# Layer 1 of the experts in seven block products for eight, in a sliding-window attention and dense expert kernel

## Chip, cores and metric

The kernel runs on 1 core of one Trainium2 chip. The metric is the device time of one execution in microseconds (us). A run is compared with runs of the kernel before on the same chip. All runs named here are of state "fast", or single executions counted as such by the measurement; no slow run is used.

## The reference

```python
def reference(...):
    attn = _attn_ref(q, k, v)        # B 8, H 8, S 576, D 64; window 128, ALiBi bias, softmax
    x = attn.transpose(0, 2, 1, 3).reshape(4608, 512)
    return _moe_ref(x, w_gate, w1, w2)

def _moe_ref(x, w_gate, w1, w2):     # N 4608 tokens, D 512, E 8 experts, F 1024
    P = np.exp(x @ w_gate - ...)     # then 8 rounds of row and column scaling (Sinkhorn)
    out = 0
    for e in range(E):
        h = np.maximum(x @ w1[e], 0.0)      # layer 1: 512 -> 1024
        out += P[:, e:e + 1] * (h @ w2[e])  # layer 2: 1024 -> 512
    return out
```

Every token passes through every expert, so nearly all of the time is matmul.

## The kernel before

Attention and most of expert 0 come first. Then 63 *steps* follow: experts 1 to 7, nine groups of 512 tokens each. A step does layer 2 of its own group and, between those products, layer 1 of the next step's group. P scales x before layer 1 (`make_xs`), which is allowed because P is positive.

Layer 2 already uses the Strassen-Winograd form: a 2x2 block product with seven block products for eight, paid for with additions of blocks. These are the sums `S` of h and `T` of w2, on VectorE. The results are gathered in an odd way: all products that several quadrants share go into quadrant (1,1), the others are kept as differences from it, and in the last expert (1,1) is added back (`settle`).

```python
def make_xs(i):                        # VectorE, two instructions of 128x1024
    ... xss[i] = xT[group] * Pb

def l1s(i, ft):                        # layer 1, direct: one eighth of a group
    psh = mps.tile([P, GT], FP32, tag="psh", bufs=3)
    for dt in range(NDT):              # 4 matmuls of 512 columns
        nc.tensor.matmul(out=psh, lhsT=w1ts[e][:, dt, P*ft : P*ft+P],
                         rhs=xss[i][:, dt, :], start=(dt == 0), stop=(dt == NDT - 1))
    nc.scalar.activation(out=hTs[i][:, ft, :], in_=psh, func=AF.Relu)

def product(i, m): ...                 # one of 7 products of layer 2: 8 matmuls of 256 columns

def gather(i, bank, rh, ch, op):
    t = quad(g, rh, ch)
    if (rh, ch) != (1, 1) and e < E - 1:         # far: ScalarE copies, a DMA adds
        st = msb.tile([P, 2, HF], FP32, tag="st", bufs=5)
        nc.scalar.copy(out=st, in_=banks[bank])
        nc.gpsimd.dma_start(out=t, in_=st, accum_op=ALU.add)
        return
    nc.vector.tensor_tensor(out=t, in0=t, in1=banks[bank], op=op)

for i, (e, g) in enumerate(steps):
    make_s(i, 1); product(i, 1); piece()         # piece(): l1s of step i + 1
    make_s(i, 2); gather(i, 0, 1, 1, ALU.add)
    product(i, 7); piece(); make_s(i, 4); gather(i, 1, 1, 1, ALU.subtract)
    product(i, 5); piece(); gather(i, 2, 1, 1, ALU.subtract)
    product(i, 6); piece(); gather(i, 3, 1, 1, ALU.add)
    make_xs(i + 2)
    # ... products 2, 4, 3 with pieces between them, gathers to the other quadrants ...
    if g == NG - 2: make_t(e + 1)                # four sums of w2, once per expert
```

The softmax here doesn't subtract the row's maximum and nothing guards it: scores larger than these inputs give would overflow.

## Time and profile before

| | before |
|---|---|
| median of 13 executions | 1089.14 us (1087.56 to 1090.73) |
| span of the profiled execution | 1086.9 us |
| before step 0 / steps 0 to 60 / the rest | 261.9 / 795.1 / 29.9 us |
| one step | 13.02 us; 13.14 us in the last seven of these steps |

A step is measured in the timeline from the start of its product 1 to the start of the next step's. The third row splits the span at product 1 of step 0 and of step 61.

The busy times on the profile's page, as time, share of the span and number of instructions:

```profile
PE 1051.8 (97%) x7675; PEld 672.5 (62%) x7675; DVE 694.2 (64%) x1072; ACT 543.2 (50%) x959; POOL 270.6 (25%) x264
```

Some of the page's costliest groups: busy time, mean ns of one, then the idle time of the engine just before them and what ended it. Matmuls are pipelined, so the busy time divided by the count is nearer their cost than the mean.

```profile
L580 ACT ACTIVATE hT<-psh 128x512 f16<-128x512 f32 x504 | 302.3, 600 | 424.3 <-PE psh L573 422.7
L573 PE MATMUL psh<-xs,w1t 128*128 128x512 f16 x2016 | 506.3, 379 | 0.2 <-DVE xs L560 0.2
...
L648 DVE TENSOR_TENSOR acc_lo<-acc_lo,M 128x512 f32<-128x512 f32 x186 | 127.2, 684 | 61.6 <-PE M L631 61.6
L560 DVE TENSOR_TENSOR xs<-xT,Pb 128x1024 f16<-128x1024 f16 x126 | 148.2, 1219 | 0.8 <-DMA Pb<-PTd 0.8
```

ScalarE and VectorE wait for TensorE here; the layer-1 matmuls waited 0.2 us in all. Product 1 of three successive steps in the timeline (start, length, engine, line, operation; every second row with this name is product 2 and is left out):

```profile
600.45 1.04 PE L631 MATMUL M<-w2t,hT 128*128 128x256 f16 x8
...
613.47 1.04 PE L631 MATMUL M<-w2t,hT 128*128 128x256 f16 x8
...
626.49 1.04 PE L631 MATMUL M<-w2t,hT 128*128 128x256 f16 x8
```

They lie 13.02 us apart. The table by windows for one step gives each engine's busy time in it, with its number of instructions, then granted clock, DMA share and GB/s:

```profile
601.39:614.41 13.02, 13.02 (x90) 8.60 (x89) 7.43 (x10) 6.12 (x11) 3.57 (x4) 1.00 0.50 83
```

The columns are PE, PEld, DVE, ACT, POOL. TensorE is busy all the time, VectorE for 7.43 us.

### The profile page before, as it was taken

Reading aid. Unit: us, or ns where it says so; the run is one execution under the profiler, and the core shown is the slowest. Engines: PE = TensorE matmul, PEld = TensorE weight load, DVE = VectorE, ACT = ScalarE, POOL = GpSimd, SP = SyncE. Lnnn points to the kernel's source line nnn. Section 1 sums busy time; section 2 is a strip of 40 time slices with the busy share of each in tenths; the row PEclk is TensorE's granted clock in tenths of the full one; section 3 lists DMA queues with packets and bytes.
Section 4 is the critical chain, followed back from the end, with each engine's and each line's share of the span. In section 5 each row is a group of like instructions: output and inputs, shape, how many; then the busy total and the mean of one; then the engine's idle time right before and its main releaser. Section 6 shows DMA issues by size and latency. Waiting matters only on the chain.

```text
span 1086.9 us, 18767 instructions
## 1 busy us (share of the span) xinstructions
PE 1051.8 (97%) x7675; PEld 672.5 (62%) x7675; DVE 694.2 (64%) x1072; ACT 543.2 (50%) x959; POOL 270.6 (25%) x264
## 2 busy tenths in 40 slices
PE   4999999899999999999999999999999999999996
PEld 2555555445666666666666666666666666666664
DVE  5877676556666755565555655565556555667885
ACT  3566666455666544444444444444444444443331
POOL 6333320010223332223222322332222322220000
PEclk9999999899999999999999999999999999999999
DMA  9977871415444595448544765559444944443323
GB/s 168 153 75 78 76 71 9 71 21 121 83 83 79 91 160 87 81 78 146 88 78 79 123 124 84 85 84 162 78 78 78 154 80 83 83 61 105 104 92 96
DMA packets 123334, 101.36 MB, mean 93 GB/s; under 512 B 46288, under 2 KB 107120, under 8 KB 123248
## 3 DMA queue, kind: packets, MB, share of 16 engines
q0 software_dynamic: 107968, 73.44, 50.5%
q1 hardware_dynamic: 14848, 26.34, 7.9%
q8 instruction: 60, 0.98, 0.4%
q10 hardware_dynamic: 432, 0.39, 0.1%
q14 instruction: 26, 0.21, 0.1%
HBM read 79.02 MB, written 9.58 MB: 82 GB/s over the span
## 4 chain that ended last, share of the span: by engine, by line
PE 93%; DVE 2%; DMA 1%; ACT 1%; issue 1%; DVEq 0%; POOL 0%; ACTq 0%; SPq 0%; POOLq 0%
PE psh L573 40%; PE M L631 35%; PE psh L110 6%; PE psy L124 5%; PE psS L218 3%; PE psN L266 2%; ACT pt L226 1%; PE psT_q L187 1%; PE psT_k L187 1%; DMA qf<-in_q_dram 1%; PE psXT L306 1%; DVE xsb L275 0%; DMA PTd<-PT_sb 0%; DVE acc_hi L648 0%; DVE QZ L206 0%
## 5 line engine op out<-in xcount | busy, mean ns | idle before, releaser
L580 ACT ACTIVATE hT<-psh 128x512 f16<-128x512 f32 x504 | 302.3, 600 | 424.3 <-PE psh L573 422.7
L573 PE MATMUL psh<-xs,w1t 128*128 128x512 f16 x2016 | 506.3, 379 | 0.2 <-DVE xs L560 0.2
L573 PEld LDWEIGHTS <-w1t 128*128 128x128 f16 x2016 | 197.3, 98 | 145.7 <-issue 0.5
L631 PEld LDWEIGHTS <-S 128*128 128x128 f16 x2016 | 197.3, 98 | 75.7
L597 DVE TENSOR_TENSOR S<-hT 128x1024 f16<-128x1024 f16 x126 | 86.8, 689 | 198.8 <-ACT hT L580 198.8
L646 POOL DMA_DIRECT2D acc_lo<-st x108 | 128.8, 1211 | 339.4 <-ACT st L645 338.7
L631 PEld LDWEIGHTS <-hT 128*128 128x128 f16 x1512 | 147.9, 98 | 59.3 <-issue 3.1
L648 DVE TENSOR_TENSOR acc_lo<-acc_lo,M 128x512 f32<-128x512 f32 x186 | 127.2, 684 | 61.6 <-PE M L631 61.6
L560 DVE TENSOR_TENSOR xs<-xT,Pb 128x1024 f16<-128x1024 f16 x126 | 148.2, 1219 | 0.8 <-DMA Pb<-PTd 0.8
L631 PE MATMUL M<-w2t,S 128*128 128x256 f16 x1008 | 130.6, 273 | 0.0
L631 PE MATMUL M<-w2t,hT 128*128 128x256 f16 x1008 | 130.6, 273 | 0.0
L631 PE MATMUL M<-T,S 128*128 128x256 f16 x1008 | 130.5, 273 | 0.0
L646 POOL DMA_DIRECT2D acc_hi<-st x54 | 64.4, 1204 | 170.1 <-ACT st L645 167.7
L645 ACT COPY st<-M 128x512 f32<-128x512 f32 x162 | 93.9, 580 | 0.0
L648 DVE TENSOR_TENSOR acc_hi<-acc_hi,M 128x512 f32<-128x512 f32 x93 | 63.6, 684 | 29.3 <-PE M L631 29.0
L226 ACT ACTIVATE pt<-psS 128x1024 f16<-128x1024 f32 (+2 forms) x80 | 68.2, 852 | 17.9 <-PE psS L218 16.8
L110 PE MATMUL psh<-xT,w1t 128*128 128x512 f16 x288 | 72.2, 393 | 1.6 <-ACT P_sb L298 1.1
L124 PE MATMUL psy<-w2t,hT 128*128 128x512 f16 x288 | 66.6, 379 | 0.8 <-ACT P_sb L298 0.8
L631 PE MATMUL M<-T,hT 128*128 128x256 f16 x504 | 65.3, 273 | 1.2 <-DVE acc_hi L648 1.2
L117 ACT ACTIVATE hT<-psh 128x512 f16<-128x512 f32 x72 | 43.1, 598 | 27.1 <-PE psh L110 26.4
L218 PE MATMUL psS<-QZ,KT 128*128 128x512 f16 (+2 forms) x160 | 46.6, 374 | 8.0 <-ACT pt L226 7.2
L234 DVE TENSOR_TENSOR pt<-pt,maskT 128x1024 f16<-128x1024 f16 (+2 forms) x80 | 46.0, 575 | 5.6 <-ACT pt L226 5.4
(61 smaller groups left out, 639.3 us busy)
## 6 DMA issues: line engine op xcount, KB each, us to landing
acc_lo<-st POOLq DMA_DIRECT2D x108, 256.0 KB, 3.9
Pb<-PTd SPq DMA_DIRECT2D x63, 256.0 KB
acc_hi<-st POOLq DMA_DIRECT2D x54, 256.0 KB, 3.9
w2t<-in_moe_w_dram POOLq DMA_DIRECT2D x8, 1024.0 KB, 15.9
w1t<-in_moe_w_dram POOLq DMA_DIRECT2D x7, 1024.0 KB, 9.8
out_dram<-acc_lo SPq DMA_DIRECT2D x48, 128.0 KB
kf<-in_k_dram POOLq DMA_DIRECT2D x16, 288.0 KB, 6.1
qf<-in_q_dram POOLq DMA_DIRECT2D x16, 288.0 KB, 7.0
```

Source lines behind the costliest of these rows:

```text
L110: nc.tensor.matmul(out=psh, lhsT=w1t[:, dt, P * ft : P * ft + P], rhs=xT[:, dt, GT * g : GT * g + GT], start=(dt == 0), stop=(dt == NDT - 1),)
L124: nc.tensor.matmul(out=psy, lhsT=hT[:, ft, P * ms : P * ms + P], rhs=w2ts[e][:, ft, :], start=(ft == 0), stop=(ft == NFT - 1),)
L218: nc.tensor.matmul(out=ps[0:nk, jj, :, 0:nq], lhsT=KT[:, 2 * half + jj, k0 : k0 + nk], rhs=QZ[:, 2 * half + jj, :, k0 : k0 + nq],)
L226: nc.scalar.activation(out=pt[0:nk, :, 0:nq], in_=ps[0:nk].rearrange("p a b q -> p (a b) q")[:, :, 0:nq], func=AF.Exp, scale=scale,)
L560: nc.vector.tensor_tensor(out=xss[i][:, 2 * d2 : 2 * d2 + 2, :], in0=xT[:, 2 * d2 : 2 * d2 + 2, GT * g : GT * g + GT], in1=Pb.unsqueeze(1) ...
L573: nc.tensor.matmul(out=psh, lhsT=w1ts[e][:, dt, P * ft : P * ft + P], rhs=xss[i][:, dt, :], start=(dt == 0), stop=(dt == NDT - 1),)
L580: nc.scalar.activation(out=hTs[i][:, ft, :], in_=psh, func=AF.Relu)
L597: nc.vector.tensor_tensor(out=t, in0=a, in1=b, op=op)
L631: nc.tensor.matmul(out=ps[:, ms, :], lhsT=a[:, kt, P * ms : P * ms + P], rhs=b[:, kt, :], start=(first and ms == 0 and kt == 0), stop=(kt ...
L645: nc.scalar.copy(out=st, in_=banks[bank])
L646: nc.gpsimd.dma_start(out=t, in_=st, accum_op=ALU.add)
L648: nc.vector.tensor_tensor(out=t, in0=t, in1=banks[bank], op=op)
```

## The change

Layer 1 gets the Strassen-Winograd form too. Its cost per step on TensorE falls from 32 matmuls of 512 columns to 56 of 256, seven eighths. The price: three differences of x and one made in place, per step; three sums of w1 and one in place, per expert; and inside each half of layer 1, two copies by ScalarE (one from PSUM to PSUM) and two additions from PSUM by VectorE. Around it much is rearranged so that VectorE keeps up. The core of the diff, with cuts:

```diff
-        def l1s(i, ft): ...                       # direct layer 1
+        def make_xd(i, n):                        # differences of x, 128x512 fp16
+            out, a, b = {
+                1: (xd[:, 0], x_quad(i, 0, 1), x_quad(i, 0, 0)),
+                2: (xd[:, 1], x_quad(i, 1, 1), xd[:, 0]),
+                3: (x_quad(i, 0, 1), x_quad(i, 1, 1), x_quad(i, 0, 1)),
+                4: (xd[:, 2], x_quad(i, 1, 0), xd[:, 1]),
+            }[n]
+            nc.vector.tensor_tensor(out=out, in0=a, in1=b, op=ALU.subtract)
+        def make_ws(e, n): ...                    # four sums of w1, 128x1024 fp16
+        def l1_product(i, dp, m): ...             # 4 matmuls of 256 columns
+        def l1_chunk(i, n):
+            dp, c = divmod(n, 4)
+            if c == 0:
+                l1_product(i, dp, 1)              # bank la
+                nc.scalar.copy(out=lbanks["lb"], in_=lbanks["la"])
+                l1_product(i, dp, 5)              # bank ld
+                m5 = msb.tile([P, 2, T2], FP32, tag="st", bufs=NST)
+                nc.scalar.copy(out=m5, in_=lbanks["ld"])
+            elif c == 1:
+                l1_product(i, dp, 6)              # adds onto the copy in lb
+                l1_product(i, dp, 2)
+                nc.vector.tensor_tensor(out=lbanks["lc"], in0=lbanks["lb"], in1=m5s[i], op=ALU.add)
+                l1_relu(i, dp, lbanks["la"], 0, 0)
+            elif c == 2:
+                l1_product(i, dp, 7)
+                l1_product(i, dp, 3)
+                nc.vector.tensor_tensor(out=m5s[i], in0=lbanks["lb"], in1=m5s[i], op=ALU.add)
+                l1_relu(i, dp, lbanks["lc"], 0, 1); l1_relu(i, dp, m5s[i], 1, 1)
+            else:
+                l1_product(i, dp, 4)
+                l1_relu(i, dp, lbanks["lb"], 1, 0)
...
-                st = msb.tile([P, 2, HF], FP32, name=f"st{bank}_{e}_{g}", tag="st", bufs=5)
+            st = msb.tile([P, 2, HF], FP32, name=f"st{bank}_{e}_{g}", tag="st", bufs=NST)  # NST = 6
...
+            # the last expert too goes by ScalarE and DMA, except its last two steps;
+            # make_t and make_ws are spread over three steps at each expert change;
+            # rescaling and rebasing of expert 0 are spread over the first steps;
+            # P is transposed and sent earlier, within expert 0's layer 1
```

The copy of product 5 (`m5`) shares the staging buffers `st` with the far adds.

## The prediction

> **What bounds the kernel now.** TensorE. It is busy for 97% of the span (the page's busy times), the chain of waits that ended last is 93% PE, and from 300 to 1000 us PE is busy 100.00 of every 100 us at a granted clock of 1.00 (the table by windows). That stretch holds steps (7 experts x 9 token groups = 63). In the timeline one step takes 13.02 us (S1 of two successive steps: 601.39 and 614.41). Its PE part: 32 matmuls of 512 columns for layer 1, eight in 1.73 us, so 6.93 us; 56 of 256 columns for layer 2, eight in 0.87 us, so 6.08 us. VectorE is 58 to 67% busy there, ScalarE 43 to 58%.
>
> **What the change does.** Layer 2 already uses seven block products for eight; now layer 1 does too. Per step, 32 matmuls of 512 columns become 56 of 256.
> - Removed: 6.93 - 56 x 0.1085 = 0.85 us of PE per step, about 53 us in all, entirely on the critical path. Layer 2's narrower matmuls cost no more per column (0.1085 against 0.2165 us).
> - Added on VectorE, per step: four 128x512 fp16 differences of x (0.41 us each, estimated from the mask multiplies of 1024 elements, 0.683 us, and 768, 0.550 us) and four fp32 128x512 additions from PSUM (like the gather: 0.684 us). Back to back, an instruction starts 0.60 us after one of 0.684 us, so the load becomes about 11.1 us in a step of 12.15 us: 91%.
> - Added on ScalarE: four copies of 0.58 us per step; load about 8.5 of 12.15 us.
> - Added per expert: four 128x1024 sums of w1 on VectorE, 0.69 us each.
> - Moved: P is sent earlier; first-expert rescaling is spread out; last-expert adds mostly go through ScalarE and DMA.
>
> The Trainium skill ("VectorE: DVE Perf Modes", Mode 2x_1P) says tensor_tensor on packed 16-bit data gives two results per cycle; this trace agrees: 1024 fp16 elements take 0.69 us, 512 fp32 elements 0.68 us.
>
> **How much arrives.** I walked one ordinary step through the queues with these durations. Each PSUM addition gates a later TensorE product into the same bank, with 0.3 to 0.4 us to spare; VectorE idles about 1 us per step. So ordinary steps should stay bound by PE at about 12.15 us. Given back: six expert changes (VectorE full for three steps each) 3 to 6 us; the last expert, two settling additions per step, 3 to 4 us; the last-but-one step, seven extra VectorE operations, 3 to 4 us; the first step's layer 1, half of it with nothing to interleave, 2 to 3 us. Together 12 to 15 of 53 us.
>
> **Predicted time: 1050 us, range 1041 to 1067.** Chances: faster by over 2% 0.87, within 2% 0.11, slower 0.02.
>
> **What would show it.** Steps of 12.1 to 12.3 us in the middle; PE still 98 to 100% busy from 300 to 950 us; about 9190 PE matmuls; VectorE busy about 960 us (over 90%), ScalarE about 700 us; PE waits on VectorE under 0.3 us per ordinary step, larger at expert changes and in the last expert.
>
> **What would make it wrong.** PSUM-to-PSUM additions slower than 0.684 us, or dependent VectorE operations that don't overlap: then VectorE becomes the limit, steps take 12.4 to 13 us, and the time 1055 to 1085 us. POOL's descriptor work could hold up the DMA adds and the staging buffers. A lower granted clock would also cost.

## The result

| | before | after |
|---|---|---|
| median | 1089.14 us, 13 executions | 1058.33 us, 8 executions (1053.95 to 1060.54) |
| span of the profiled execution | 1086.9 us | 1053.0 us |
| before step 0 / steps 0 to 60 / the rest | 261.9 / 795.1 / 29.9 us | 261.5 / 758.7 / 32.8 us |
| ordinary step | 13.02 us | 12.22 us |
| TensorE / VectorE / ScalarE busy | 1051.8 / 694.2 / 543.2 us | 1003.3 / 923.3 / 692.1 us |

The ratio is 0.9709, 95% interval 0.9693 to 0.9725. Such a ratio is the mean time of one kernel's fast runs over that of the other's of the same rounds, so it is not quite the ratio of the medians above. The outputs are correct. The profiled execution took 1054.86 us and is one of the quicker ones.

The same lines of the page, after:

```profile
PE 1003.3 (95%) x9187; PEld 815.3 (77%) x9187; DVE 923.3 (88%) x1566; ACT 692.1 (66%) x1249; POOL 322.8 (31%) x310
...
L563 DVE TENSOR_TENSOR xs<-xT,Pb 128x1024 f16<-128x1024 f16 x126 | 153.3, 1217 | 0.0
L620 PE MATMUL la<-xs,w1t 128*128 128x256 f16 x1008 | 151.2, 273 | 0.7 <-DVE xs L563 0.7
...
L656 DVE TENSOR_TENSOR lc<-lb,m 128x512 f32<-128x512 f32 x126 | 87.9, 697 | 33.2 <-PE lb L620 28.7
L735 DVE TENSOR_TENSOR acc_lo<-acc_lo,M 128x512 f32<-128x512 f32 x163 | 110.8, 680 | 0.2
```

VectorE's idle time before the gathers (L735) has shrunk from 61.6 to 0.2 us; what it still waits for is mainly the layer-1 bank `lb` of the first PSUM addition. Product 1 of three ordinary steps:

```profile
623.46 1.04 PE L723 MATMUL M<-w2t,hT 128*128 128x256 f16 x8
...
635.68 1.04 PE L723 MATMUL M<-w2t,hT 128*128 128x256 f16 x8
...
647.91 1.04 PE L723 MATMUL M<-w2t,hT 128*128 128x256 f16 x8
```

Now 12.22 and 12.23 us lie between them, 112 matmuls of 0.109 us. The table by windows for three kinds of step: an ordinary one, the second at an expert change, and one of the last expert.

```profile
635.68:647.91 12.23, 12.23 (x114) 10.96 (x112) 11.26 (x19) 8.22 (x17) 3.60 (x3) 1.00 0.57 93
598.17:611.01 12.84, 12.54 (x114) 10.86 (x112) 12.63 (x22) 8.76 (x18) 6.57 (x6) 1.00 1.10 174
957.69:970.19 12.50, 12.43 (x115) 10.96 (x113) 12.28 (x21) 8.32 (x17) 3.60 (x3) 1.00 0.73 148
```

In the ordinary step TensorE is busy throughout and VectorE is idle for 0.97 us. In the other two VectorE has hardly any idle time left and TensorE waits. At an expert change that wait looks like this in the timeline (square brackets: idle time before, and what ended it):

```profile
606.88 0.42 DVE L584 TENSOR_TENSOR xd<-xs 128x512 f16<-128x512 f16 x1
607.22 0.68 DVE L703 TENSOR_TENSOR T<-w2t,T 128x1024 f16<-128x1024 f16 x1
607.96 1.03 PE L723 MATMUL M<-T,hT 128*128 128x256 f16 x8 [0.30 <-DVE T L703]
```

The third sum of w2 is late because VectorE's queue is full. From the step starts, the time lost against 12.22 us in the profiled execution is: 2.9 us in step 0 (15.11 us); 7.3 us at six expert changes (0.9 us at four of them, 2.2 at the first, 1.5 at the last); 1.35 us in five steps of the last expert (12.50 us each); 0.3 us in the other steps of expert 1; and about 1 us in three steps that follow a step with weight loads. The rest, from the start of step 61 on, is 2.9 us longer than before.

### The profile page after: what moved, and what is told of

Same layout as the page of the kernel before. It is cut to its first block, busy times and chain, and to the rows that moved or that the text cites. A ratio compares the mean times of both kernels' runs of the same rounds, so it can differ in the third digit from the quotient of the medians.

```text
span 1053.0 us, 22956 instructions
## 1 busy us (share of the span) xinstructions
PE 1003.3 (95%) x9187; PEld 815.3 (77%) x9187; DVE 923.3 (88%) x1566; ACT 692.1 (66%) x1249; POOL 322.8 (31%) x310
## 5 line engine op out<-in xcount | busy, mean ns | idle before, releaser
L635 ACT ACTIVATE hT<-lc 128x512 f16<-128x512 f32 x126 | 75.4, 598 | 138.5 <-PE lc L620 131.0
L620 PEld LDWEIGHTS <-ws 128*128 128x128 f16 x1512 | 147.3, 98 | 20.4 <-DVE ws L598 1.7
L620 PE MATMUL la<-xs,w1t 128*128 128x256 f16 x1008 | 151.2, 273 | 0.7 <-DVE xs L563 0.7
L723 PE MATMUL M<-T,hT 128*128 128x256 f16 x1008 | 130.6, 273 | 4.9 <-DVE T L703 2.4
L635 ACT ACTIVATE hT<-la 128x512 f16<-128x512 f32 x126 | 75.6, 600 | 72.7 <-PE la L620 72.7
L656 DVE TENSOR_TENSOR lc<-lb,m 128x512 f32<-128x512 f32 x126 | 87.9, 697 | 33.2 <-PE lb L620 28.7
L735 DVE TENSOR_TENSOR acc_lo<-acc_lo,M 128x512 f32<-128x512 f32 x163 | 110.8, 680 | 0.2
L663 DVE TENSOR_TENSOR m<-lb,m 128x512 f32<-128x512 f32 x126 | 86.2, 684 | 2.8 <-PE lb L620 2.8
L635 ACT ACTIVATE hT<-lb 128x512 f16<-128x512 f32 x126 | 75.8, 602 | 8.3 <-PE lb L620 7.2
L635 ACT ACTIVATE hT<-m 128x512 f16<-128x512 f32 x126 | 78.7, 625 | 1.7
L647 ACT COPY lb<-la 128x512 f32<-128x512 f32 x126 | 71.8, 570 | 9.0 <-PE la L620 1.6
```

Of the source, the lines that this page charges most:

```text
L620: nc.tensor.matmul(out=ps[:, f, :], lhsT=a[:, kt, f0 : f0 + P], rhs=b[:, kt, :], start=(first and f == 0 and kt == 0), stop=(kt == 1), ski ...
L635: nc.scalar.activation(out=hTs[i][:, f0 : f0 + 2, T2 * th : T2 * th + T2], in_=src, func=AF.Relu)
L647: nc.scalar.copy(out=lbanks["lb"], in_=lbanks["la"])
L656: nc.vector.tensor_tensor(out=lbanks["lc"], in0=lbanks["lb"], in1=m5s[i], op=ALU.add)
L663: nc.vector.tensor_tensor(out=m5s[i], in0=lbanks["lb"], in1=m5s[i], op=ALU.add)
L723: nc.tensor.matmul(out=ps[:, ms, :], lhsT=a[:, kt, P * ms : P * ms + P], rhs=b[:, kt, :], start=(first and ms == 0 and kt == 0), stop=(kt ...
```

## Experiments

Twelve runs were made, of eleven new kernels and of the changed one again. Each was timed against the kernel before. My theory: ordinary steps are still bound by TensorE, VectorE has about 1 us to spare in each, and what is missing was lost where VectorE has extra work. The rivals: VectorE, 92% busy in an ordinary step (11.26 of 12.23 us), now sets the pace everywhere; or the gain came from the rearranging and not from the seven products.

### direct_l1: the new schedule with the old layer 1

```diff
         def l1_chunk(i, n):
-            ...                                  # seven products
+            psh = mps.tile([P, GT], FP32, name=f"psh_{e}_{g}_{n}", tag=LB[n % 4])
+            for dt in range(NDT):
+                nc.tensor.matmul(out=psh, lhsT=w1ts[e][:, dt, P * n : P * n + P],
+                                 rhs=xss[i][:, dt, :], start=(dt == 0), stop=(dt == NDT - 1))
+            nc.scalar.activation(out=hTs[i][:, n, :], in_=psh, func=AF.Relu)
         # make_xd and make_ws return at once
```

> The changed schedule with layer 1 as before: 32 direct matmuls of 512 columns per step, no x differences, no w1 sums, no additions from PSUM. If the seven-product form of layer 1 makes the gain, the steps go back to 13.02 us and the time to 1085 to 1092 us, ratio 0.995 to 1.003. Rival: the gain comes from what was moved (P sent earlier, the last expert's adds given to ScalarE and DMA, rescaling spread): then a good part of the 31 us stays and the time is under 1075 us. Here a settle of the tail may even cost 2 to 4 us.

Measured: correct, 1090.04 us, ratio 1.0003 (0.9981 to 1.0024). One step by windows:

```profile
601.07:614.09 13.02, 13.02 (x90) 8.61 (x89) 7.95 (x11) 6.70 (x12) 4.80 (x5) 1.00 0.61 101
```

All 61 steps take 13.02 us, those of the last expert too (13.14 us before). The part after step 61 is 32.0 us, against 29.9 us before; up to TensorE's last matmul it is 21.3 us, against 20.7 us. So the rearranging alone brings nothing in total. The rival that credits the rearranging falls. No run has the new layer 1 in the old order, so whether the rearranging was needed is not shown.

### light_x: VectorE relieved (wrong results on purpose)

```diff
         def make_xd(i, n):
+            if i > 1:
+                xds[i] = xds[i % 2]
+                return
```

> Wrong results on purpose: the differences of x are made for the first two steps only, so 1.3 to 1.6 us of VectorE work leaves every later step, and TensorE does the same products. If ordinary steps are bound by TensorE, they stay at 12.22 us, and only the places where VectorE is full gain: about 0.9 us at each of six expert changes and 0.27 us in each of the last expert's steps, together 6 to 10 us, time 1047 to 1052 us. Rival: VectorE, at 93% busy, sets the pace; then every step shortens by 0.5 us or more and the time falls below 1030 us.

Measured: wrong as intended, 1051.91 us, ratio 0.9654 (0.9634 to 0.9673). One ordinary step:

```profile
623.12:635.34 12.22, 12.22 (x114) 10.96 (x112) 9.91 (x15) 8.31 (x17) 3.59 (x3) 1.00 0.59 95
```

VectorE's load fell from 11.26 to 9.91 us and the step stayed at 12.22 us: VectorE does not set the pace of an ordinary step. The steps at four of the expert changes became 12.22 or 12.23 us, and so did those of groups 2 to 7 of the last expert. That shows where a full VectorE cost time. But five steps, each the one after the step in which the next expert's weights were loaded, took 0.3 to 2.0 us more, 6.1 us in all, which I had not expected. One of them:

```profile
840.27 0.57 ACT L650 COPY lb<-la 128x512 f32<-128x512 f32 x1
...
843.59 0.59 ACT L654 COPY m<-ld 128x512 f32<-128x512 f32 x1 [2.75 <-DMA acc_lo<-st]
844.21 0.70 DVE L659 TENSOR_TENSOR lc<-lb,m 128x512 f32<-128x512 f32 x1 [3.17 <-ACT m L654]
...
844.96 0.60 PE L623 MATMUL lb<-xs,w1t 128*128 128x256 f16 x4 [1.86 <-DVE lc L659]
```

ScalarE cannot copy product 5, because its staging buffer is still held by a DMA add that has not landed. VectorE waits for the copy and TensorE for VectorE. This is the shared buffer pool of the diff. DMA adds took 4.9 us (median) and up to 14.2 us to land in this run.

### heavy1 and heavy2: VectorE loaded

```diff
+            def extra():
+                if 2 <= e <= 6 and 1 <= g <= 6:          # 30 ordinary steps
+                    for _ in range(1):                   # heavy2: 2
+                        nc.vector.tensor_tensor(out=P_sb, in0=P_sb, in1=P_sb, op=ALU.max)
             gather(i, 0, 1, 1, ALU.add)
+            extra()
...
                 gather_far(i, 0, 0, 0)
+            extra()
             chunk(5)
```

> Two idle-filling operations of VectorE (0.46 us each alone, about 0.38 us back to back) added to each of 30 ordinary steps (token groups 1 to 6 of experts 2 to 6), one before each first PSUM addition, where I saw VectorE wait. If VectorE has about 0.9 us to spare per step, these steps stay at 12.22 to 12.30 us and the time moves by 0 to +3 us. Rival (VectorE sets the pace): each step grows by 0.76 us, +23 us.

> Twice as many: four such operations, about 1.5 us, in each of the 30 ordinary steps. More than the spare time of about 0.9 us, so the steps should grow by 0.4 to 0.7 us each, +12 to +21 us. Rival (VectorE sets the pace): +1.5 us per step, +46 us. If VectorE had much more to spare than I read: no change.

Measured: heavy1 1059.50 us, ratio 0.9721 (0.9694 to 0.9749); heavy2 1077.97 us, ratio 0.9891 (0.9864 to 0.9919); both correct. One loaded step of each by windows, heavy1 first:

```profile
636.66:648.88 12.22, 12.22 (x114) 10.96 (x112) 11.98 (x21) 8.21 (x17) 3.60 (x3) 1.00 0.59 93
```

```profile
634.59:647.55 12.96, 12.59 (x114) 10.93 (x112) 12.72 (x23) 8.39 (x16) 3.59 (x3) 1.00 0.60 95
```

In heavy1 the loaded steps stay at 12.22 or 12.23 us, but for two that follow weight loads (12.76 and 12.57 us; the changed kernel has such steps too). Each extra operation moves what follows by 0.48 us, so the two of a step add 0.96 us and just fill VectorE's waits. In heavy2 most loaded steps take 12.97 us, 0.75 us more, where I had expected 0.4 to 0.7 us. There two extra operations push the next addition 0.86 us back:

```profile
637.72 0.94 DVE L800 TENSOR_TENSOR P_sb<-P_sb 128x288 f32<-128x288 f32 x2
638.58 0.69 DVE L656 TENSOR_TENSOR lc<-lb,m 128x512 f32<-128x512 f32 x1
639.33 0.60 PE L620 MATMUL lb<-xs,w1t 128*128 128x256 f16 x4 [0.21 <-DVE lc L656]
```

So 1.72 us were added per step, and 0.75 us came out. The spare time was about 0.97 us, which is VectorE's idle time in the ordinary step of the changed kernel, as the prediction's walk had it ("about 1 us"). Past that, TensorE stands before exactly the product that the PSUM addition gates. Together, light_x, heavy1 and heavy2 rule out that VectorE sets the pace in ordinary steps, and show that it is close to doing so.

### spread and st7: the late DMA adds

```diff
-            if g == 0 and 1 < e < E - 1:          # spread: whole w1 and w2 loads in group 0
-                load_w1(...); load_w2(...)
+            if 0 <= g < 4 and 1 < e < E - 1:      # a quarter of each in groups 0 to 3
+                nc.gpsimd.dma_start(out=w1ts[e + 1][:, g : g + 1], in_=...)
+                nc.gpsimd.dma_start(out=w2ts[e + 1][:, 2 * g : 2 * g + 2], in_=...)
```

```diff
-        NST = 6                                   # st7
+        NST = 7
...
-                t = msb.tile([P, KT2, T2], FP16, name=f"S{n}_{e}_{g}", tag=f"S{n}")
+                t = msb.tile(..., tag="S2" if n == 2 else "S34")   # S3 and S4 share a buffer
```

> The changed kernel, correct, with the loads of an expert's w1 and w2 cut into four parts each, one pair in each of the steps of token groups 0 to 3, in place of two whole loads in group 0. Theory: the changed kernel's runs (1054 to 1060.5 us) differ because a DMA add behind a weight load holds a staging buffer, for which ScalarE's copy of the fifth product, and then TensorE, wait (in the trace 1 us of such waits in the profiled run of the changed kernel, more in the slower ones). Then the waits of ScalarE on DMA go away, the median falls to 1053 to 1056 us and the runs lie within 3 us. Rival: the spread has another cause (clock, chip): median 1057 to 1060 and the spread as before.

> The changed kernel, correct, with seven staging buffers in place of six (room made by letting two of the layer-2 sums share one buffer). If staging buffers held by late DMA adds cost time, one more takes most of the wait: ScalarE's waits on DMA under 2 us, median 1054 to 1057 us. Rival: no effect of the number of buffers, 1057 to 1060 us. If the shared buffer adds a wait in ordinary steps, they would show over 12.23 us.

Measured, both correct: spread 1057.28 us (1056.49 to 1057.78), ratio 0.9708 (0.9695 to 0.9722); st7 1054.91 us (1053.93 to 1055.88), ratio 0.9687 (0.9674 to 0.9700). In the changed kernel ScalarE waited for DMA before the copy of product 5 for 3.3 us in all. In spread no such wait is left and the longest landing is 8.7 us, where the changed kernel has 13.2 us; in st7 none is left before that copy, though 2.9 us remain before the copies of the far adds (I had expected under 2 us). Both shorten steps 0 to 60 by 0.8 us, from 758.7 to 757.9 us. So the mechanism is right, but it is worth about 1 us. The median of spread missed my range and lies in the rival's, though its four runs lie within 1.3 us. In its profiled execution the time before step 0 was 265.0 us, where st7 had 262.0 us and the changed kernel 261.5 us, with the same program up to there. Most of the spread between runs is therefore not the late adds. The traces show where these 3.5 us arise: early in the attention, in spread's stretch from 40 to 47 us, the granted clock is 0.50 and a 128x512 matmul takes 0.62 us, where the changed kernel has 1.00 and 0.38 us; the 201st to the 400th matmul take 22.2 us in spread and 19.7 us there. The matmuls of 0.62 us end at 39 to 40 us in four of the fourteen traces (the changed kernel, st7, best3, settle_pool) and at 47 to 50 us in the other ten. What ends them is not shown.

### settle_pool: the last expert's additions on GpSimd

```diff
-            nc.vector.tensor_tensor(out=t, in0=t, in1=quad(g, 1, 1), op=ALU.add)
+            eng = nc.vector if g == NG - 1 else nc.gpsimd
+            eng.tensor_tensor(out=t, in0=t, in1=quad(g, 1, 1), op=ALU.add)
```

> The changed kernel, correct, with the last expert's settling additions on GpSimd in place of VectorE, but for the last token group. If the last expert's steps take 12.50 us because VectorE is full, they fall to 12.23 to 12.30 us, and the last step starts earlier by up to 2.6 us: 2 to 5 us in all, median 1053 to 1056 us. Rival: GpSimd is too slow at it or hinders VectorE; then the VectorE operations beside it take longer and the steps stay at 12.5 us or grow.

Measured: correct, 1076.92 us, ratio 0.9889 (0.9870 to 0.9909). The rival was right, and by more than I had thought. The steps of the last expert take 13.65 to 17.14 us once these additions begin. From the timelines of VectorE and of GpSimd:

```profile
979.22 0.68 DVE L688 TENSOR_TENSOR S<-hT 128x1024 f16<-128x1024 f16 x1
980.00 1.57 DVE L688 TENSOR_TENSOR hT<-hT 128x1024 f16<-128x1024 f16 x1
981.60 3.91 DVE L688 TENSOR_TENSOR S<-hT 128x1024 f16<-128x1024 f16 x1
```

```profile
978.62 3.83 POOL L744 DMA_DIRECT2D acc_lo<-st  x3
981.04 3.91 POOL L749 TENSOR_TENSOR acc_lo<-acc_lo 128x512 f32<-128x512 f32 x2
```

The same operation on VectorE takes 0.68 us alone and 3.91 us beside two GpSimd additions. The Trainium skill ("SBUF — State Buffer", the section "SBUF: two separate sides") says that a VectorE operation with two SBUF inputs and a GpSimd operation that reads SBUF take a shared pair of ports as an exclusive lock and that the loser "fully blocks". This trace agrees. But the ports are only part of the loss in the profiled execution: steps 0 to 60 take 8.5 us more than in the changed kernel, and about as much is lost before step 0. There GpSimd's first `partition_all_reduce`, part of the scaling of P, starts only after an idle time of 9.91 us (3.05 us in the changed kernel), TensorE waits 5.22 us for P, and for some 7 us after that its granted clock is low (0.57 in the stretch from 240 to 248 us). Of the fourteen traces only this one has it; whether it comes from the edit is not shown.

### start_tail: two orders on VectorE

```diff
+        make_xs(1, 0); make_xd(1, 1)               # x of step 1, in the gaps of step 0's layer 1
         for n in range(3, 8):
             l1_chunk(0, n)
+            # ... make_xs(1, 1) after chunk 4, the other differences after chunks 5 and 6
         make_s(0, 3)
-        make_x(1)
...
-            if i == NS - 2: settle(g, 0, 1); store(...); settle(g - 1, 0, 1); store(...)
+            # the same two settles in the last step, before product 5 and before product 3
```

> The changed kernel, correct, with two orders on VectorE changed: x of the second step is made in the gaps of the first layer 1, and the second column's settling of the last two groups comes after the sums that TensorE waits for in the last step. If the first step's 15.1 us and the tail's 32.8 us after the start of the last-but-one step come from VectorE's order, the first falls to 12.8 to 13.5 us and the second to 31 to 32 us: 2 to 4 us less, median 1054 to 1057 us. Rival: other waits take their place, and the time stays.

Measured: correct, 1055.55 us (1054.95 to 1060.79), ratio 0.9704 (0.9683 to 0.9725). Step 0 fell from 15.11 to 12.23 us, so its loss was VectorE's order. The tail did not reach the expected 31 to 32 us: 33.4 us, against 32.8 us. Yet its TensorE part, up to the last matmul, fell from 22.2 to 21.3 us: a wait of 0.90 us before product 5 of the last step went away, and product 4 then waited 1.55 us for VectorE in place of 1.39 us. The stores after the last matmul took 12.1 us here, and 10.6 and 12.3 us in two traces of the changed kernel. This spread hides the gain, so the end of the span does not tell whether this half helped.

### again, best1 and best2

`again` is the changed kernel unaltered. `best1` joins st7 and the first half of start_tail. `best2` adds to it:

```diff
+            if g < NG - 2:                          # settle: groups 0 to 6 by DMA
+                nc.gpsimd.dma_start(out=t, in_=quad(g, 1, 1), accum_op=ALU.add)
+                return
...
-            if i == NS - 2:
+            if i == NS - 2 and (rh, ch) != (0, 0):  # one more far add in step 61
```

> The changed kernel once more, unaltered, as the mark for the two beside it on the same chip: 1054 to 1060 us. Its trace should again have ordinary steps of 12.23 us, 12.5 and 12.8 us in the two steps before an expert change takes effect, 12.5 us in the last expert, and a few waits of ScalarE on late DMA adds.

> Correct: seven staging buffers and x of the second step made in the gaps of the first layer 1, both of which helped alone (step 0 fell from 15.11 to 12.23 us; the waits on late adds nearly went). They touch different places, so they should add: 4 to 6 us under the unaltered changed kernel beside it, 1051 to 1053 us. If the two only shift the same wait, 1054 to 1056 us.

> As the one before, and correct, with the settling additions of the last expert's first seven groups given to DMA adds, in place of VectorE, and one more far add of the last-but-one step by ScalarE and DMA. The attempt on GpSimd failed because VectorE was held beside it; a DMA add was not seen to hold it. If VectorE is what stretches the last expert, its steps fall from 12.50 to 12.23 us and the tail after the start of the last-but-one step from 32.8 to 30 to 32 us: 2 to 4 us more, 1048 to 1051 us. Rival: the DMA adds land too late, the stores wait, and the end moves out: 1052 us or more.

Measured, all correct: again 1059.72 us, ratio 0.9735 (0.9716 to 0.9754); best1 1053.28 us, ratio 0.9678 (0.9663 to 0.9694); best2 1072.94 us, ratio 0.9857 (0.9841 to 0.9873).

best1 is 6.4 us under the changed kernel on the same chip. In the traces its steps 0 to 60 take 754.7 us, where again has 759.2 us. These 4.5 us are the 2.9 us of step 0 and the 1.6 us that steps after weight loads lose in again: the two gains add, and best1 beats both kernels.

In best2 three steps of the last expert after the first settling fell from 12.50 to 12.22 or 12.23 us, as the theory of a full VectorE has it, and then two took 14.92 and 14.23 us. SyncE's queue in the timeline (the count is the number of DMAs issued in the stretch):

```profile
982.34 11.07 SPq L77 DMA_DIRECT2D out_dram<-acc_lo  x8
993.52 2.26 SPq L554 DMA_DIRECT2D Pb<-PTd  x1
995.89 14.13 SPq L77 DMA_DIRECT2D out_dram<-acc_lo  x8
1010.12 0.38 SPq L554 DMA_DIRECT2D Pb<-PTd  x1
1010.61 42.00 SPq L77 DMA_DIRECT2D out_dram<-acc_lo  x24
1052.78 14.23 SPq L77 DMA_DIRECT2D out_dram<-acc_hi  x16
```

A load of P stands behind eight stores, and these fall behind. VectorE then waits for P:

```profile
1002.36 1.23 DVE L563 TENSOR_TENSOR xs<-xT,Pb 128x1024 f16<-128x1024 f16 x1 [3.39 <-DMA Pb<-PTd]
```

The span ends at 1070.8 us with stores, although TensorE had finished at 1043 us.

### best3: the stores one step later

```diff
+                if 0 <= g - 2 < 4:                  # on top of best1
+                    for blk in range(4 * g - 8, 4 * g - 4):
+                        store(blk, engs=(nc.sync, nc.gpsimd if g - 2 == 3 else nc.sync))
+                if g - 1 < 4:
+                    # settle group g - 1 by two DMA adds
+                else:
+                    put_out(g - 1)
```

> Correct: seven staging buffers, x of the second step in the gaps of the first layer 1, and the settling of token groups 0 to 3 of the last expert by DMA adds, but with the stores of a group one step later, when these adds have landed, and one far add of the last-but-one step by ScalarE and DMA. In the attempt before, steps fell to 12.23 us until the stores, which wait in order in one queue for late DMA adds, held back the loads of P behind them. If that is the cause, the steps of groups 1 to 4 are 12.23 us, no step is over 12.6 us, and the time is 1051 to 1053 us, 1 to 2 us under the version without it. Rival: DMA adds of this kind cost the other traffic even when nothing waits for them: steps over 13 us again, 1055 us or more.

Measured: correct, 1062.17 us, ratio 0.9747 (0.9729 to 0.9764). The expectation on the steps held for groups 1 to 5, which take 12.22 or 12.23 us, but step 61 takes 13.59 us, where best1 has 12.56 us: TensorE waits 0.88 us there for a PSUM addition, since VectorE had stood 1.00 us before a settling addition until a DMA add landed. Steps 0 to 60 take 753.8 us, in best1 754.7 us, so TensorE gains about 1 us up to step 61 and loses it again in that step. (Product 1 of step 61 begins at 1016.5 us, where best1 has 1019.9 us, but 2.5 us of this lie before step 0.) The expectation on the time failed: the end comes 44.5 us after that, where best1 needs 33.5 us. The table by windows from 980 to 1000 us, best3 first, then best1:

```profile
980.00:1000.00 20.00, 20.00 (x185) 17.94 (x184) 18.45 (x30) 13.44 (x25) 10.80 (x9) 1.00 1.00 185
```

```profile
980.00:1000.00 20.00, 19.87 (x181) 17.45 (x180) 19.74 (x34) 12.73 (x24) 6.80 (x6) 1.00 0.82 173
```

The DMA share (last column but one) is 1.00, where best1 has 0.82, and the stores issue late and slowly in best3, 28 in 45.75 us:

```profile
995.07 45.75 SPq L77 DMA_DIRECT2D out_dram<-acc_lo  x28
1040.94 15.70 SPq L77 DMA_DIRECT2D out_dram<-acc_hi  x16
```

So relieving VectorE shortened the steps that it had filled, gained TensorE nothing in total, and the stores came last and later. Why they came later is not shown. The DMA adds may have taken room on the DMA engines; the issuing queue, which works in order, may be the limit; and the edit itself moves the stores of four groups one step (12.2 us) later. The share does not decide it: it reads 1.10 at the expert change of the changed kernel above, so 1.00 is not a full engine by itself. No run separates the three.

## Why the prediction was right, and where its sizes were off

The time, 1058.33 us, lay in the stated range (1041 to 1067) and the direction was right.

- *"ordinary steps should stay bound by PE"*: shown. 1.35 us less VectorE work (light_x) and 0.96 us more (heavy1) both left the step at 12.22 us.
- *"VectorE idles about 1 us per step"*: shown: 0.97 us idle in the table by windows, and 0.97 us absorbed in heavy2. VectorE's load, forecast as about 11.1 us, is 11.26 us.
- *"0.85 us of PE per step, about 53 us"*: measured 0.80 us per step, so about 50 us over 62 steps (an estimate from the step). I took 0.1085 us for a matmul of 256 columns; the steps show 0.109 us, in layer 2 too. The Trainium skill ("TensorE: Matmul & The Clock Gate", the section "Back-to-back issue gap") gives N / 2.4 + 2.5 ns for the isolated gap between matmuls of N columns; the estimate from it for 256 columns is 109.2 ns, and this trace agrees (0.109 us). This mis-sized term is 3 of the missing microseconds.
- *"six expert changes ... 3 to 6 us"*: 7.3 us in the profiled execution. light_x shows that it is VectorE, since most of it vanished there.
- *"the last expert ... 3 to 4 us"*: 1.35 us in the steps. The cause was right (12.22 us where the settling left VectorE, in best2 and best3); the size was too large.
- *"the first step's layer 1 ... 2 to 3 us"*: 2.9 us, and start_tail took it away.
- *"the last-but-one step ... 3 to 4 us"*: the part after step 61 is 2.9 us longer, though TensorE has 0.8 us less to do in it. Up to TensorE's last matmul it takes 20.7 us in the kernel before, 21.3 us in direct_l1 and 22.2 us in the changed kernel: 0.6 us come with the new order, 0.9 us more with the new layer 1. The rest is stores. These took 9.2 us in the kernel before, and 10.6 and 12.3 us in two traces of the changed kernel (the second is again), so one trace does not size their share.
- *"could hold up the DMA adds and the staging buffers"*: right as a risk, by another way than I named: adds behind weight loads land late. It is about 1 us in the changed kernel and 6.1 us in light_x. It was in no sum.
- *VectorE "over 90%"* of the span: 923.3 us, 88%. ScalarE about 700: 692.1. PE matmuls about 9190: 9187.

The profiled execution, at 1054.86 us, lies 4.9 us over the predicted median. The matmul term, the expert changes and the late adds, less the last expert, make up about that. Here luck helped: the expert changes cost more than forecast and the last expert less, and these two errors nearly cancel. The other 3.5 us to the median are the spread between executions. The trace of again, whose profiled execution took 1058.85 us, is 4.1 us longer than the changed kernel's: 1.8 us before step 0, where its matmuls of 0.62 us last until 48 us (39 us there), 0.5 us in steps 0 to 60, and 1.8 us after them, in the stores. What sets either is not shown.

## What to carry to other kernels

When arithmetic moves from the busiest engine to one that is nearly full, the average step can still show the whole gain; look for the loss in the steps that carry something extra, and measure the spare time by adding work until the step grows. A buffer pool shared by a quick use and one that ends with a DMA ties the quick one to the slowest landing. Before relieving an engine with another, ask what the two share: GpSimd shared ports with VectorE, and behind the DMA adds of best2 and best3 came later stores, which ended the kernel.

## What the Trainium skill lacked or had wrong

- "TensorE: Matmul & The Clock Gate", "Back-to-back issue gap": it gives about 131 ns per matmul for a sustained stream with N = 512. Here eight matmuls of 512 columns, each with its weight load, take 1.73 us, 216 ns each, at a granted clock of 1.00. The "isolated" formula of the same section fits the sustained stream at 256 and 512 columns (estimates from it 109.2 and 215.8 ns, start to start here 109.1 and 215.8 ns).
- "VectorE: DVE Perf Modes", "The DRAIN you can't avoid": it says that the next operation does not start until the pipe is empty, and points to another section for one that starts earlier. Here a 128x512 fp32 addition of 0.68 us is followed 0.60 us later by an independent one. No page that I read gives the distance to an operation that reads the result of the one before: here it starts 0.72 us after it (two sums S in the changed kernel, 624.66 and 625.38 us).
- "SBUF — State Buffer": the lock is described, and that it is held for the whole instruction, but not what that comes to for additions on both engines. One VectorE operation of 0.68 us took 3.91 us beside two GpSimd additions.
- No page that I read gives the time to landing of an accumulating DMA within SBUF. Here 256 KB took 3.9 us (median) in the kernel before, 4.8 us in the changed kernel, and up to 13.2 us there and 14.2 us in light_x. With the weight loads split (spread) the longest was 8.7 us.
